# A transformer block on one core: the second chunk of x loaded ahead of wk and w_mod, silu on GpSimd, a copied w_phi product, and a new order

## The chip, the cores and the metric

The kernel runs on one core of a Trainium2 chip. The metric is the device time in microseconds, the median of several runs. The core has five instruction streams that wait for each other through semaphores: TensorE (PE, with its weight loads PEld), VectorE (DVE), ScalarE (ACT), GpSimd (POOL) and SyncE (SP), which here issues nearly all DMAs.

## The reference

Only the computation is shown; all inputs and outputs are bf16, and S = 2048 tokens, D = 512, 32 heads of 16, F = 1376.

```python
mod = (silu(c) @ w_mod).reshape(1, 6, 1, 512)        # sa, ca, ga, sb, cb, gb
h = layernorm(x) * (1 + ca) + sa
x = x + ga * A(h)
h = layernorm(x) * (1 + cb) + sb
x = x + gb * (silu(h @ w_gate) * (h @ w_up)) @ w_down

def A(h):
    q, k, v = heads(h @ wqkv)
    pq, pk = q @ w_phi, k @ w_phi                    # one 16x16 matrix for each head
    phi_q = concat(softmax(pq), softmax(-pq)); phi_k = concat(softmax(pk), softmax(-pk))
    kv = sum over tokens of phi_k^T v; z = sum over tokens of phi_k
    return ((phi_q @ kv) / (phi_q @ z + 1e-6)) @ wo
```

## The kernel before

The 2048 tokens are 4 chunks (x_c0 to x_c3) of 4 tiles of 128 tokens; the 16 tiles are numbered through. All weights stay in SBUF once loaded.

Preparation. x, wk, w_phi and w_mod are loaded by `later` (L288), one DMA on SP each. silu(c) is computed in `f_silu` (L453) with an Exp before it (L459). Its product with w_mod (`mod_cols`, L465) gives the shift and scale columns modA (and later modB and the gates). w_phi is folded into wk and wq: `f_phx` (L495) spreads the heads' matrices into PSUM, one product with a mask (L502) makes the block matrix BD of it, and `fold_phi` (L508) turns wk by TensorE (L519), evacuates the turned pieces WT (L523), multiplies them with BD (L530), and evacuates the result over wk (L533, L534). wq is turned by DMA instead. First layernorm (`first_norm`, L542): statistics by VectorE (L348, L349), the reciprocal root either by Ln and Exp on ScalarE (L377, L378) or by GpSimd (L381, L382), a small reduction (L384), and the normalization on one of three engines (L392, L396, L398). Tiles 0 to 5 are turned by TensorE (L563, L414), later ones by DMA (L577); the evacuation applies modA and gives hT (L566, L567 for tiles 0 and 1, L422 for tiles 2 to 5).

First phase. For each tile `k_tile` computes K (L619) and V (L623) into PSUM banks. Two Exp of K on ScalarE (L634) give e, VectorE sums them (S, L640), R is the reciprocal, va is V times R (L650), GpSimd scales e (L657), and eight small matmuls add to kv (L663). `q_tile` does the like for Q (L686, L690, L694, L701), whose result goes through a DMA transpose (pT, L705).

Second phase. For each tile kv is applied (L824), the denominators are inverted (A, L827), the result o is turned (oT), multiplied with wo (L857, whose columns were scaled by the gate at L780), added to x, normalized again and turned; then the gated feed-forward network (L909, L916 to L926, L955) and the product with w_down (L987), the last sum (L997, L1001) and the store (L1007).

The order of all this isn't the order of the code. Each piece is registered by `pl.op` with the engine or engines that may do it and a duration. A list of numbers, `ORDER`, fixes in which sequence they are placed and which engine does each: a number is four times the operation's index plus the choice among its engines. From the durations `Plan.run` computes planned starts, and the instructions are issued sorted by them, so each engine's own sequence is fixed in the program:

```python
for x in ORDER:
    o = self.ops[x // 4]
    o.alt = o.alts[x % 4]
...
for o in sorted(self.ops, key=lambda o: (o.start, o.n)):
    if o.eng == "PE":
        fill(last, o, fns)
```

`fill` (L1037) puts matmuls of ones (L1054) into planned gaps of TensorE; their results are not used. Six PSUM banks of 512 columns (`one_ps`) are shared by nearly all products, so a product may have to wait until an earlier one in its bank has been read.

Of the kernel before, what the change touches and what calls it, by code (L numbers as in the profile page):

```python
# [14 lines left out]
P = 128  # L15
# [5 lines left out]
D = 512  # L21
# [14 lines left out]
def fm_size(m):  # L36
# [5 lines left out]
DMA_LN1 = 6  # L42
FILL_FROM, FILL_TO, FILL = 1.3, 90.0, 0.85
# [3 lines left out]
    0, 4, 48, 188, 72, 80, 8, 12, 16, 76, 20, 60, 52, 204, 228, 84, 56, 220, 172, 64, 208, 89, 92, 98, 156, 232, 176, 224, 24, 212, 104, 180, 193,  # L47
    28, 161, 236, 100, 184, 240, 196, 108, 217, 40, 246, 112, 164, 148, 116, 120, 124, 153, 36, 250, 32, 200, 268, 140, 168, 132, 128, 276, 316,
    252, 272, 68, 260, 144, 280, 136, 520, 264, 256, 324, 285, 320, 524, 328, 44, 424, 488, 428, 288, 560, 528, 464, 380, 492, 333, 600, 568, 294,
    298, 480, 432, 300, 472, 484, 336, 564, 468, 476, 368, 496, 342, 308, 532, 436, 346, 536, 304, 500, 541, 392, 440, 348, 608, 312, 384, 548, 445,  # L50
    604, 572, 510, 388, 828, 768, 404, 577, 452, 772, 544, 872, 372, 820, 376, 812, 776, 1344, 584, 506, 552, 513, 940, 518, 448, 460, 408, 412,
    804, 362, 358, 456, 396, 580, 780, 366, 944, 816, 864, 354, 904, 596, 824, 400, 868, 556, 808, 640, 832, 636, 612, 785, 792, 592, 836, 840, 908,
    788, 617, 644, 588, 1020, 876, 704, 800, 1340, 858, 1028, 648, 1024, 950, 796, 624, 881, 916, 620, 652, 416, 629, 962, 953, 888, 632, 860, 958,
    853, 1060, 921, 736, 656, 912, 1032, 846, 1188, 884, 712, 708, 900, 928, 716, 964, 1037, 744, 1228, 1268, 740, 1276, 924, 660, 1044, 850, 896,
    1308, 748, 1304, 933, 1040, 664, 1192, 1232, 893, 1200, 1360, 420, 1052, 936, 1318, 668, 720, 988, 1272, 1056, 993, 1240, 1196, 1049, 752, 1352,
    1205, 1325, 1212, 1328, 1208, 1224, 1280, 1313, 1236, 1322, 1245, 1252, 1336, 1356, 1220, 1285, 1364, 1248, 1264, 724, 1520, 1600, 1217, 1524,
    1369, 1292, 1604, 1528, 1260, 1348, 1004, 1560, 728, 1257, 1288, 1372, 1297, 1532, 1300, 1008, 1376, 1608, 1612, 1384, 1537, 1544, 1540, 1564,
    1816, 1388, 1617, 1620, 1640, 968, 1552, 1381, 1644, 1572, 1556, 1064, 1549, 1624, 1652, 1577, 1632, 1568, 1124, 1584, 1332, 1132, 1128, 1648,
    1580, 1592, 1596, 972, 1657, 1136, 976, 672, 1660, 1068, 996, 1636, 1589, 756, 1664, 1629, 1672, 732, 1072, 1669, 1676, 676, 1824, 980, 760,
    1828, 1092, 680, 1001, 1832, 1100, 984, 1680, 1836, 684, 1856, 1860, 1096, 1076, 1812, 1864, 1156, 1104, 1108, 1160, 1808, 1744, 2164, 1820,  # L60
    2168, 764, 1080, 1084, 2172, 1868, 1872, 1392, 1164, 1876, 1400, 2176, 688, 1748, 1424, 1112, 1116, 1880, 2180, 1688, 2184, 1488, 692, 1088,
    1884, 1396, 1712, 1888, 1120, 2416, 1684, 2188, 1140, 696, 1168, 1432, 1892, 2420, 700, 1752, 1776, 2424, 1716, 1898, 1172, 1456, 1492, 1144,
    1496, 1148, 1012, 1720, 1908, 1428, 1912, 1464, 2428, 1900, 1904, 2432, 2216, 1176, 2192, 2436, 2220, 2224, 2196, 2012, 2440, 1784, 2228, 1936,
    1152, 2016, 1460, 1180, 1780, 2200, 1016, 2204, 1952, 1500, 1916, 2020, 2232, 1940, 1944, 1956, 2237, 1948, 2444, 2208, 2024, 1404, 1960, 1184,
    2214, 2468, 2028, 1436, 2512, 2516, 1964, 1920, 1968, 2240, 1504, 2032, 2520, 2257, 1988, 2472, 2250, 1972, 2524, 1992, 1408, 1976, 2448, 1440,
    2246, 2253, 2296, 1980, 2528, 2316, 1924, 2452, 2036, 1984, 2260, 2040, 2532, 1444, 2304, 1412, 1448, 1416, 1452, 2352, 2536, 2044, 2300, 2456,
    1928, 2476, 2324, 2320, 1508, 1420, 1788, 2048, 2460, 2280, 2328, 1692, 2936, 1512, 1932, 2052, 2264, 2308, 2480, 2284, 2940, 2540, 2268, 2272,
    2288, 2944, 2056, 1516, 2332, 2544, 2484, 2924, 2360, 2564, 2292, 1848, 2928, 2340, 2932, 1792, 2948, 2064, 2568, 2548, 2312, 2060, 2336, 1724,
    2552, 2490, 2368, 2068, 2344, 2088, 2465, 1996, 2356, 2104, 2572, 2576, 2348, 2392, 1696, 2364, 2976, 2580, 2000, 2128, 2096, 1468, 1472, 2585,
    2072, 2556, 1728, 2980, 1476, 2492, 2984, 2372, 2276, 2506, 2112, 1732, 2124, 1481, 2952, 1756, 2988, 2561, 2588, 2510, 2132, 3032, 3036, 2605,  # L70
    1700, 1484, 3040, 2594, 2956, 1796, 2376, 2396, 2092, 2498, 1704, 2400, 2601, 2108, 2501, 2597, 2992, 1736, 2136, 2076, 3020, 2380, 2704, 2808,
    3024, 2080, 2720, 3028, 2960, 2404, 2116, 2997, 2964, 2668, 2648, 2816, 2100, 3044, 2724, 1708, 2652, 1760, 2728, 1740, 2732, 2968, 2676, 2974,
    2664, 2672, 3072, 2680, 3048, 3076, 3444, 1764, 2656, 2712, 2812, 2736, 3080, 3000, 2608, 2120, 3448, 2756, 1801, 3452, 2820, 3432, 3052, 3084,
    1804, 3056, 2760, 2744, 3060, 2140, 2660, 2764, 2824, 2628, 2612, 3436, 2616, 3064, 3088, 2408, 2144, 3013, 3006, 3440, 2700, 2620, 2084, 3094,
    3009, 2772, 2768, 2708, 2740, 1768, 3069, 3456, 2632, 3540, 3096, 2004, 2780, 1853, 2776, 3544, 2784, 2716, 3460, 2148, 3105, 2152, 3484, 3101,
    3017, 3548, 3488, 3492, 2792, 2684, 1772, 2636, 2688, 2748, 3464, 3114, 3528, 3532, 3110, 2752, 2788, 3536, 2692, 3468, 2640, 3552, 2796, 3116,
    3472, 2800, 3268, 3264, 3212, 3220, 2008, 3272, 2696, 3120, 2804, 3136, 3140, 3496, 3208, 3500, 3276, 3144, 3556, 3560, 3172, 3244, 3564, 3216,
    3476, 3568, 2624, 3482, 3180, 3148, 3300, 2900, 3580, 3572, 3584, 3176, 3252, 2156, 3224, 2904, 3308, 2876, 3124, 2852, 3588, 3506, 3184, 2644,
    2412, 3592, 2880, 2884, 2385, 2908, 3508, 3284, 3152, 2912, 3188, 3304, 2856, 3292, 3280, 3248, 3596, 3312, 3602, 3525, 3192, 3256, 3578, 3288,
    3604, 3200, 2860, 3617, 1844, 3296, 3196, 3128, 3228, 3514, 3613, 3236, 3320, 3316, 2388, 3156, 3608, 3521, 3620, 1841, 3518, 3204, 2864, 3160,  # L80
    3132, 3716, 3164, 2888, 3232, 3720, 3260, 3168, 3240, 3664, 3644, 3324, 3328, 3648, 3684, 3728, 3384, 3332, 3692, 3652, 2160, 3336, 3724, 3388,
    3672, 2828, 3360, 3408, 3392, 3412, 2868, 2832, 3364, 3396, 3656, 3340, 3788, 3624, 3416, 3344, 2917, 3732, 3368, 2872, 3401, 2893, 2836, 2840,
    3796, 2920, 3628, 3632, 3668, 3420, 3756, 3636, 3404, 3700, 2844, 3808, 3708, 2848, 3676, 3348, 3680, 3688, 3704, 3712, 3792, 3764, 3752, 3776,
    3760, 3812, 3372, 3696, 3772, 3800, 3740, 3816, 3736, 3376, 3768, 2896, 3780, 3824, 3804, 3660, 3424, 3828, 3380, 3744, 3748, 3784, 3844, 3848,
    3892, 3640, 3836, 3820, 3916, 3920, 3832, 3840, 3852, 3924, 3353, 3896, 3900, 3356, 3868, 3872, 3876, 3928, 3856, 3940, 3944, 3948, 3861, 3960,
    3964, 3968, 3933, 3904, 3428, 3909, 3864, 3880, 3952, 3936, 3912, 3885, 3972, 3976, 3956, 3888,
# [122 lines left out]
def kernel(  # L209
# [78 lines left out]
    def later(dst, src, w, kb):  # L288
        pl.op("XBAR", w=list(w), us=0.5, kb=kb, fn=lambda: nc.sync.dma_start(dst, src))
# [25 lines left out]
    nc.gpsimd.memset(mhalf[:], -0.5)  # L315
    eps_t = const.tile([P, 1], FP32, name="eps")
# [114 lines left out]
    later(x_ch[0][:], x_v[0], bx[0:4], 400)  # L431
# [32 lines left out]

    def mod_cols(mt, n0, bw):  # L465
# [69 lines left out]

    hT = [[attn.tile([P, CW], BF16, name=f"hT_{c_i}_{j}") for j in range(KD)] for c_i in range(NCH)]
    bhT = [[[Buf() for _ in range(KD)] for _ in range((2, 2, 1, 1)[c_i])] for c_i in range(NCH)]

    bxn1 = {}
    bmodA = None  # L540

# [552 lines left out]
```

## Time and profile before

| | |
|---|---|
| time, median of 3 runs | 199.34 us (199.23 to 199.69) |
| time of the profiled execution | 199.18 us |
| its span in the profile | 197.4 us |
| granted TensorE clock | 1.00 |
| TensorE busy | 192.4 us, 97% of the span |
| VectorE, ScalarE, GpSimd busy | 136.3, 108.9, 126.0 us |
| moved by DMA | 24.16 MB |

The span reaches from the first to the last recorded instruction; the time also holds what lies around it. A row of the timeline gives the start in us, the duration of the group in us, the engine, the line, the operation, what it writes and reads, the shape, and how many instructions were merged. In brackets stands how long the engine had been idle and what released it. Ends of matmuls are modelled, so I count a row of matmuls by its starts. Busy columns of the windows view are PE, PEld, VectorE, ScalarE and GpSimd, then the granted clock, the DMA engines' share and the GB/s moved.

### The profile page before, as it was taken

What the parts mean: (1) busy time and instruction counts of PE and PEld (TensorE: products, weight loads), DVE (VectorE), ACT (ScalarE), POOL (GpSimd) and SP (SyncE); (2) the same over time, 40 slices, a digit from 0 to 9 for tenths busy, and PEclk for the clock granted to TensorE, in tenths of its full rate; (3) what the DMA queues carried; (4) which work ended last, traced back from release to release, by engine and by line L of the source; (5) the groups of instructions that cost most, each with busy time, mean ns of one, the idle gap of its engine ahead of it and who ended that gap; (6) DMA issues with size and microseconds to landing.
All of it is one profiled execution on the core that took longest, in us unless ns stands there. A gap on an engine that the chain in (4) does not pass through costs nothing.

```text
span 197.4 us, 4080 instructions
## 1 busy us (share of the span) xinstructions
PE 192.4 (97%) x1494; PEld 108.1 (55%) x1494; DVE 136.3 (69%) x268; ACT 108.9 (55%) x247; POOL 126.0 (64%) x207
## 2 busy tenths in 40 slices
PE   7999999999999999999999999999999999999993
PEld 2754555555754777967664555554444544544452
DVE  5999999999999899998973873844234203241453
ACT  2499999999769974366452452633145330134300
POOL 1469999999997667686763777657746420139200
DMA  6999789899928570836509157150370001021112
GB/s 203 334 381 151 129 201 355 186 310 392 203 53 162 107 151 13 167 66 110 99 14 188 37 100 82 30 130 0 66 103 20 27 0 53 3 66 40 47 38 76
DMA packets 51141, 24.16 MB, mean 122 GB/s; under 512 B 42449, under 2 KB 47922, under 8 KB 51122
## 3 DMA queue, kind: packets, MB, share of 16 engines
q1 hardware_dynamic: 50976, 23.88, 51.7%
q8 instruction: 11, 0.18, 0.4%
q14 instruction: 8, 0.07, 0.1%
q10 hardware_dynamic: 146, 0.03, 0.1%
HBM read 11.58 MB, written 2.10 MB: 69 GB/s over the span
## 4 chain that ended last, share of the span: by engine, by line
PE 93%; DMA 3%; DVE 1%; issue 1%; SPq 0%; DVEq 0%
PE one_ps L909 35%; PE one_ps L987 17%; PE one_ps L857 7%; PE one_ps L623 7%; PE one_ps L686 7%; PE one_ps L619 7%; PE one_ps L955 3%; DMA wk<-in_A_wqkv_dram 2%; PE kv_ps L663 2%; PE kv_ps L824 2%; PE kv_ps L1054 1%; DMA out_dram<-ot 1%; PE one_ps L530 1%; PE one_ps L473 1%; DVE fg L997 1%; PE one_ps L414 1%
## 5 line engine op out<-in xcount | busy, mean ns | idle before, releaser
L909 PE MATMUL one_ps<-hT,wgu_sb 128*128 128x512 bf16 (+2 forms) x480 | 74.5, 308 | 0.0
L909 PEld LDWEIGHTS <-wgu_sb 128*128 128x128 bf16 x480 | 40.3, 98 | 28.7
L916 ACT ACTIVATE sg<-one_ps 128x512 bf16<-128x512 f32 (+1 forms) x41 | 23.6, 586 | 37.2 <-PE one_ps L909 24.9
L987 PE MATMUL one_ps<-wd_sb,gu 128*128 128x512 bf16 (+1 forms) x160 | 37.8, 372 | 0.0
L925 POOL TENSOR_TENSOR gu<-usb,sg 128x512 bf16<-128x512 bf16 x19 | 22.1, 1168 | 24.2 <-ACT sg L916 12.2
L997 DVE TENSOR_TENSOR fg<-one_ps,gab 128x512 bf16<-128x512 f32 (+1 forms) x16 | 10.4, 667 | 23.8 <-PE one_ps L987 23.8
L919 DVE TENSOR_TENSOR gu<-one_ps,sg 128x512 bf16<-128x512 f32 (+1 forms) x22 | 14.2, 658 | 18.1 <-PE one_ps L909 11.1
L987 PEld LDWEIGHTS <-gu 128*128 128x128 bf16 x180 | 16.6, 98 | 16.0
L348 DVE BATCH_NORM_STATS2 st<-x_c 128x6 f32<-128x512 bf16 x32 | 21.3, 678 | 1.7 <-DMA x_c<-in_A_x_dram 1.5
L923 ACT CAST usb<-one_ps 128x512 bf16<-128x512 f32 x19 | 11.1, 586 | 18.2 <-PE one_ps L909 18.0
L640 DVE TENSOR_REDUCE S<-e 128x64 f32<-128x1024 bf16 x16 | 19.2, 1202 | 0.4 <-POOL e L657 0.2
L694 DVE TENSOR_REDUCE Sq<-eq 128x64 f32<-128x1024 bf16 x16 | 19.2, 1203 | 0.0
L690 ACT ACTIVATE eq<-one_ps 128x512 bf16<-128x512 f32 x32 | 17.1, 614 | 2.3 <-PE one_ps L686 2.2
L634 ACT ACTIVATE e<-one_ps 128x512 bf16<-128x512 f32 x32 | 17.0, 615 | 0.0
L657 POOL TENSOR_TENSOR e<-e,S 128x512 bf16<-128x512 bf16 x16 | 16.8, 1060 | 0.2
L857 PE MATMUL one_ps<-wo_sb,oT 128*128 128x512 bf16 x64 | 16.1, 379 | 0.0
L623 PE MATMUL one_ps<-wv,hT 128*128 128x512 bf16 x64 | 15.9, 379 | 0.0
L619 PE MATMUL one_ps<-wk,hT 128*128 128x512 bf16 x64 | 15.5, 379 | 0.0
L686 PE MATMUL one_ps<-wq,hT 128*128 128x512 bf16 x64 | 15.4, 379 | 0.0
L701 POOL TENSOR_TENSOR eq<-eq,Rq 128x512 bf16<-128x512 bf16 x14 | 14.8, 1059 | 0.4
L1001 POOL TENSOR_TENSOR ot<-x_c,fg 128x512 bf16<-128x512 bf16 x7 | 8.1, 1153 | 10.0 <-DVE fg L997 10.0
L860 DVE TENSOR_TENSOR x_c<-x_c,one_ps 128x512 bf16<-128x512 bf16 x16 | 10.7, 669 | 5.3 <-PE one_ps L857 5.1
(120 smaller groups left out, 279.7 us busy)
## 6 DMA issues: line engine op xcount, KB each, us to landing
wmod_sb<-in_w_mod_dram SPq DMA_DIRECT2D x2, 1024.0 KB, 7.8
out_dram<-ot SPq DMA_DIRECT2D x15, 128.0 KB, 1.9
x_c<-in_A_x_dram SPq DMA_DIRECT2D x3, 512.0 KB, 7.2
wgu_sb<-in_B_w_up_dram SPq DMA_DIRECT2D x1, 1376.0 KB, 10.9
wgu_sb<-in_B_w_gate_dram SPq DMA_DIRECT2D x1, 1376.0 KB, 13.4
wd_sb<-in_B_w_down_dram SPq DMA_DIRECT2D x1, 1280.0 KB, 7.5
wk<-in_A_wqkv_dram SPq DMA_DIRECT2D x1, 512.0 KB, 4.8
wmod_sb<-in_w_mod_dram SPq DMA_DIRECT2D x1, 512.0 KB, 5.9
```

What stands on the lines that cost most here:

```text
L348: pl.op("DVE", r=reads, w=[st6], us=0.6, fn=lambda: nc.vector.bn_stats(st6()[:], src))
L619: nc.tensor.matmul(pk()[:], lhsT=hT[c_i][k][:, cols], rhs=Wk2[:, k, :], start=(k == 0), stop=(k == KD - 1))
L623: nc.tensor.matmul(v()[:], lhsT=hT[c_i][k][:, cols], rhs=wv_sb[:, k, :], start=(k == 0), stop=(k == KD - 1))
L640: pl.op("DVE", r=[e], w=[Ss], us=1.13, fn=lambda: nc.vector.tensor_reduce(Ss()[:].rearrange("p g s h -> p (g s h)"), e()[:].rearrange("p g ...
L686: nc.tensor.matmul(pq()[:], lhsT=hT[c_i][k][:, cols], rhs=Wq2[:, k, :], start=(k == 0), stop=(k == KD - 1))
L690: pl.op("ACT", r=[pq, btab], w=[be[sg]], us=0.48, fn=lambda sg=sg: nc.scalar.activation(eq[:, :, sg].rearrange("p g h f -> p g (h f)"), pq ...
L694: pl.op("DVE", r=be, w=[Sq], us=1.13, fn=lambda: nc.vector.tensor_reduce(Sq()[:].rearrange("p g s h -> p (g s h)"), eq[:].rearrange("p g s ...
L857: nc.tensor.matmul(a()[:], lhsT=oT()[:, j0 + j, :], rhs=wo_sb[:, j, :], start=(j == 0), stop=(j == KD - 1))
L909: nc.tensor.matmul(ps_()[0:fsz, q * n:(q + 1) * n], lhsT=wgu_sb[:, k, i, m * P:m * P + fsz], rhs=h2[k], start=(k == 0), stop=(k == KD - 1))
L916: pl.op("ACT", r=[g, btab], w=[sg], us=0.08 + 0.41 * L / CW, fn=lambda: nc.scalar.activation(sg()[0:fsz, 0:L], g()[0:fsz, 0:L], ACT.Silu))
L925: pl.op("POOL", r=[usb, sg], w=[gu], us=0.17 + 0.98 * L / CW, fn=lambda: nc.gpsimd.tensor_tensor(gu()[0:fsz, 0:L], usb()[0:fsz, 0:L], sg() ...
L987: nc.tensor.matmul(fp()[:], lhsT=b()[0:fsz, c0:c0 + P], rhs=wd_[0:fsz, m, wcs], start=(m == 0), stop=(m == FM - 1))
```

## The change

The first chunk of x is loaded in two halves, and the order of the loads on SP becomes: first chunk, second chunk (in halves, as before), wk, w_phi, w_mod, third chunk, wq, fourth chunk, wv. In the kernel before it is: first chunk, wk, w_phi, w_mod, second chunk, third chunk, wq, wv, fourth chunk.

silu(c) is computed by GpSimd, as c times (1 + exp(-c)) to the power -1, from an SBUF copy of c that ScalarE makes. The spread w_phi is copied from PSUM to SBUF, and the block matrix is the product of this copy with the mask. It may be done by GpSimd or VectorE; `ORDER` takes VectorE for the copy and for the product. For tile 0 the reciprocal of the denominators may be done by ScalarE as Exp of minus Ln, and `ORDER` takes that. A function for layernorm statistics on ScalarE is added, but the tuple that would select tiles for it, `ACT_STATS`, is empty.

`ORDER` is new throughout. From it follow, among others: all four evacuations of tiles 0 and 1 on VectorE (L567) instead of one there and three on ScalarE; the reciprocal roots of tiles 0 to 7 by Ln and Exp on ScalarE instead of those of tiles 2 and 3 only; three of the turned pieces of wk evacuated by ScalarE instead of two; K of tiles 0 to 4 ahead of the first V instead of K of tiles 0 to 3; four transposes of the second chunk ahead of the first K; 23 filler matmuls instead of 26, of them two behind the first K instead of five; w_up's load behind the third transposed eq instead of behind the first.

```diff
+ACT_STATS = ()
+ACC = 0.8
+EARLY = 1
...
 ORDER = [
...
+    mone = const.tile([P, KD], FP32, name="mone")
+    nc.gpsimd.memset(mone[:], -1.0)
...
-    later(x_ch[0][:], x_v[0], bx[0:4], 400)
+    later(x_ch[0][:, 0:2, :], x_v[0][:, 0:2, :], bx[0:2], 210)
+    later(x_ch[0][:, 2:4, :], x_v[0][:, 2:4, :], bx[2:4], 190)
...
+    c_sb = const.tile([P, KD], FP32, name="c_sb")
+
+    def f_sig():
+        nc.scalar.copy(c_sb[:], cT()[:])
+        nc.scalar.activation(sig[:], cT()[:], ACT.Exp, scale=-1.0)
+
     def f_silu():
-        nc.vector.tensor_scalar_add(sig[:], sig[:], 1.0)
-        nc.vector.reciprocal(rsig[:], sig[:])
-        nc.vector.tensor_tensor(silucT[:], rsig[:], cT()[:], op=ALU.mult)
+        nc.gpsimd.tensor_scalar(sig[:], sig[:], 1.0, 1e38, op0=ALU.add, op1=ALU.min)
+        nc.gpsimd.tensor_tensor(rsig[:], sig[:], mone[:, 0:KD], op=ALU.pow)
+        nc.gpsimd.tensor_tensor(silucT[:], rsig[:], c_sb[:], op=ALU.mult)
...
-    pl.op("ACT", r=[cT], w=[bsig], us=0.1, fn=lambda: nc.scalar.activation(sig[:], cT()[:], ACT.Exp, scale=-1.0))
-    pl.op("DVE*", r=[bsig, cT], w=[bsil], us=0.5, fn=f_silu)
+    pl.op("ACT", r=[cT], w=[bsig], us=0.3, fn=f_sig)
+    pl.op("POOL", r=[bsig], w=[bsil], us=1.5, fn=f_silu)
...
-    pl.op("DVE", r=[phx], w=[bBD], us=0.6, fn=lambda: nc.vector.tensor_tensor(
-        BD[:], phx()[:].rearrange("p (j f) -> p j f", f=DH).unsqueeze(2).to_broadcast([P, KD, 8, DH]),
-        bm128[:].unsqueeze(1).to_broadcast([P, KD, 8, DH]), op=ALU.mult))
+    ph_sb = prep.tile([P, KD * DH], BF16, name="ph_sb")
+    bph = Buf()
+    pl.op([("ACT", 0.14, lambda: nc.scalar.copy(ph_sb[:], phx()[:])),
+           ("DVE", 0.13, lambda: nc.vector.tensor_copy(ph_sb[:], phx()[:]))], r=[phx], w=[bph])
+
+    def f_bd(eng):
+        eng.tensor_tensor(BD[:], ph_sb[:].rearrange("p (j f) -> p j f", f=DH).unsqueeze(2).to_broadcast([P, KD, 8, DH]),
+                          bm128[:].unsqueeze(1).to_broadcast([P, KD, 8, DH]), op=ALU.mult)
+    pl.op([("POOL", 1.05, lambda: f_bd(nc.gpsimd)), ("DVE*", 0.6, lambda: f_bd(nc.vector))], r=[bph], w=[bBD])
...
-        pl.op("DVE", r=[nd], w=[A], us=0.26, fn=lambda: nc.vector.reciprocal(A()[:], ndv()[:, :, HG:NDW]))
+        alts = [("DVE", 0.26, lambda: nc.vector.reciprocal(A()[:], ndv()[:, :, HG:NDW]))]
+
+        def fa():
+            nc.scalar.activation(A()[:], ndv()[:, :, HG:NDW], ACT.Ln)
+            nc.scalar.activation(A()[:], A()[:], ACT.Exp, scale=-1.0)
+        if n < EARLY:
+            alts.append(("ACT", 0.43, fa))
+        pl.op(alts, r=[nd] + ([btab] if n < EARLY else []), w=[A])
```

## The prediction

> **What bounds the kernel now.** I read the page first (part 1 for shares, part 4 for the chain), then the chain in order of time, then the timeline of the first 20 us, the DMA issues, and the busy time by window.
>
> ```profile
> span 197.4 us, 4080 instructions
> PE 192.4 (97%) x1494; PEld 108.1 (55%) x1494; DVE 136.3 (69%) x268; ACT 108.9 (55%) x247; POOL 126.0 (64%) x207
> PE 93%; DMA 3%; DVE 1%; issue 1%; SPq 0%; DVEq 0%
> ```
>
> TensorE is on the chain for 93% of the span. From the first K matmul on, it is a row of matmuls:
>
> ```profile
> 1.18 4.83 DMA wk<-in_A_wqkv_dram
> 10.53 0.83 PE kv_ps L1054 x4
> 12.35 1.73 PE one_ps L619 x8
> 14.16 1.73 PE one_ps L619 x8
> 16.05 0.97 PE one_ps L623 x4
> ```
>
> The chain begins with the load of wk, passes the preparation, and enters K (L619) at about 12.2 us. A 128x512 matmul is started every 0.216 us (8 in 1.73). The changed kernel issues the same matmuls apart from the fillers (L1054, products of ones that only keep the array busy). So the end is: start of the first K, plus matmul work left, plus fillers and waits after it, plus a tail whose instructions are alike in both (last matmul 193.97, span 197.4). In the timeline:
>
> ```profile
> 8.20 0.30 ACT L377 ACTIVATE ln_var<-ln_mv,eps 128x2 f32<-128x2 f32 x1
> 9.07 1.56 ACT L533 CAST wk<-one_ps 128x512 bf16<-128x512 f32 x3 [0.34 <-PE one_ps L530]
> 10.21 0.17 DVE L478 COPY modA<-one_ps 128x8 f32<-128x8 f32 x1 [0.48 <-PE one_ps L473]
> 10.51 1.50 ACT L566 ACTIVATE hT<-one_ps,modA 128x256 bf16<-128x256 bf16 x3
> 12.19 1.89 PE L619 MATMUL one_ps<-wk,hT 128*128 128x512 bf16 x8
> 15.73 0.32 PE L1054 MATMUL kv_ps<-ones 128*128 128x373 bf16 x1
> 15.99 1.02 PE L623 MATMUL one_ps<-wv,hT 128*128 128x512 bf16 x4
> 16.85 0.61 PE L414 MATMUL one_ps<-ident_b,xn 128*128 128x128 bf16 x8
> ```
>
> The first K waits for ScalarE, which evacuates wk until about 10.5 and then three of the four turned pieces of h one after the other. Counting the later starts against 0.216 us each, I find little else lost: five fillers after 12.19 (191, 373, 512, 480 and 228 columns, together 1784, that is 0.75 us), 0.10 before V at 15.99, 0.10 before the first product with wo at 58.5, and some 0.6 us in pieces. What can be won after the start is 1.5 us at most.
>
> ```profile
> wk<-in_A_wqkv_dram SPq DMA_DIRECT2D x1, 512.0 KB, 4.8
> wmod_sb<-in_w_mod_dram SPq DMA_DIRECT2D x2, 256.0 KB, 6.2
> 8.00:9.00 1.00, 1.00 (x21) 0.87 (x20) 1.00 (x6) 0.69 (x3) 0.77 (x1) 1.00 1.05 391
> 9.00:10.00 1.00, 1.00 (x34) 1.00 (x32) 0.72 (x3) 0.93 (x2) 0.77 (x2) 1.00 1.06 404
> ```
>
> wk lands at 6.0, the last quarter of w_mod at about 9.5; the queue moves 391 to 404 GB/s then (last column), without a gap.
>
> **The change part by part.**
>
> *Second chunk of x ahead.* SP's order becomes x0a, x0b, x1a, x1b, wk, w_phi, w_mod, x2, wq, x3, wv. 512 KB pass ahead of wk: 524 KB by 391 GB/s is 1.34 us. So wk lands at 7.35, w_phi at 7.5, the end of w_mod at 10.8. The bytes ahead of x2 and wq are unchanged (about 12.1 and 13.6). x3 and wv swap: wv lands where x3 did, about 17.3 instead of 15.95. SP issues take 0.4 to 0.7 us each, at most eight in flight. With the load of c as the first, the ninth waits for c and the tenth for x0a; both have landed by 4, so no issue is late.
>
> *First chunk in halves.* One issue more (0.45 us on SP). The first half should land near 3.5 instead of 4.1. The Trainium skill ("DMA: Bandwidth & Descriptors", sections "Anatomy of one DMA" and "Measured") speaks against it: it gives a DMA (measured on the GpSimd path) a fixed cost of about 2 us and asks for 1 MiB or more. The row says otherwise here: quarters of w_mod of 256 KB landed 0.7 us apart in the filled queue, which is their bytes at the rate above. By the rule taken serially, the half would add up to 2 us to all loads behind it (first K near 14.7); by the row, nothing. I take the row, since the fixed part is latency that lies under the transfers ahead.
>
> *silu on GpSimd.* Three VectorE instructions go (138+178+157 ns, 0.47 us); ScalarE gains a copy of c (0.17). GpSimd gets an add (0.23, row L381), a pow (0.72 for 128x2, L382; this one is 128x4, so 0.7 to 0.9) and a product (0.2, L332). It starts near 3.9 and ends by 5.3. Its reader, w_mod's products, waits for w_mod until 9.5, so it costs nothing; without that cover it would cost 0.9 us more than VectorE's version. Queued behind it on GpSimd are the masks and the first normalization, which can't start before 6.8.
>
> *w_phi's block matrix.* A copy of 128x64 on VectorE (bound 0.13 to 0.3 by the small copies; I take 0.15) and a product from SBUF, still on VectorE. The old product from PSUM took 0.673. The nearest row with two SBUF inputs is L701 on VectorE: 1011 ns. The skill ("GPSIMD Engine Reference", "Specifications") says that VectorE contends with GpSimd for SBUF when it has two SBUF inputs. The page gives no price, so the row sets it: between 0.67 and 1.01 us, I take 1.0. It ends near 9.4; ScalarE reaches wk only at 10.0. So either value gives the same sum.
>
> *Start of K, new order.* ScalarE decides. The second group of wk's turned pieces is ready for it at 8.5 (7.35, two groups of 0.23, w_phi's 0.45 between, a handover of 0.2, a little issue). Then: two WT copies of 0.48, a Ln/Exp pair 0.53 (0.30+0.20 and the gap), two wk copies of 0.48 (three in 1.44 by starts), a second pair 0.53: 11.48. VectorE waits for this pair in the reduction in front of the h pieces: handover 0.2, 0.14, then the two pieces at 0.33 (0.41 less the overlap seen between VectorE starts): 12.48. Handover 0.18: first K at 12.66, 0.47 later than 12.19. w_mod's last product (10.8) gives modA by 11.5, earlier than that. All four pieces of tiles 0 and 1 are now on VectorE. ScalarE does tiles 2 and 3 meanwhile, done near 13.8; K needs them at 14.2. Tiles 4 and 5 are done by 16.6, before K reaches them at 16.7.
>
> *What comes back.* Four transposes of the second chunk now lie ahead of the first K: 8 took 0.45 by starts, so -0.22. Fillers after the first K: 512 and 219 columns, 731 for 1784: -0.44. The wait for wv: five K tiles now come first, so V is due at 17.5, after 17.3: -0.10. At the first wo, 1.17 us instead of 0.87 of other matmuls lie under the copy of oT: -0.10. The reciprocal of tile 0's denominators by Ln and Exp on ScalarE costs 0.52 (0.266+0.256, rows L644 and L645) against 0.34, in front of a VectorE product; 1.6 us of other matmuls lie over both: nothing, or 0.2 if they don't suffice.
>
> *GpSimd's row.* A second row must keep up: GpSimd works from the first normalizations of later tiles to the last product with e, and the last kv matmuls stand right behind it.
>
> ```profile
> 14.88 3.79 POOL L398 TENSOR_SCALAR xn<-x_c,ln_mv,ln_nmr 128x512 bf16<-128x512 bf16 x5
> 51.85 1.06 POOL L657 TENSOR_TENSOR e<-e,S 128x512 bf16<-128x512 bf16 x1
> ```
>
> By starts, that row is 37.6 us of work and 0.4 idle. In the new order eight normalizations are done ahead, and from the first one of x2 to the last product with e there are 34.6 us (normalization 0.75, product 1.02, the small ones about 0.2). It starts when VectorE has reduced x2's statistics. That reduction is queued behind the sum S of the first K tile, which waits for its Exp: ScalarE is at 15.6, S ends at 16.9, statistics of x3 take 0.6, the reduction 0.15: 17.65. 17.65+34.6+0.4 = 52.65 against 52.9: -0.25. VectorE has about 1 us less in this phase, ScalarE 0.3 more; there I enter nothing, with -0.6 to +1.5 for the range.
>
> *Weights.* w_up's load is now queued behind the third transposed eq on SP instead of ahead of it. Its transfer takes 11 us, its reader starts near 67; the third eq is ready before 50 by GpSimd's row. It costs nothing unless it is issued after 55.
>
> Sum: to the last kv the array's own row gives +0.47 -0.22 -0.44 -0.10 = -0.29 and GpSimd's -0.25; the later one counts. With the wait at wo: -0.25 -0.10 = -0.35. The profiled execution took 199.18 (span 197.4 and 1.78 around it), 0.16 below the median of 199.34. 199.18 - 0.35 = 198.83; on the median's level 198.99, given as 199.0.
>
> **The rivals.** *Slower: preparation follows wk.* If ScalarE's row from wk to the h pieces shrinks by nothing, the first K is late by the whole 1.34: +1.34 -0.22 -0.44 -0.20 = +0.48, 199.8. For it: the chain starts at wk, and this order puts two Ln/Exp pairs between the copies. Against: three h pieces (1.35) leave ScalarE ahead of the first K. It decides once the first K is later than about 13.05.
>
> *Slower: GpSimd late.* The first Exp now ends near 15.6 instead of 14.7, and x2's normalization hangs on it. If ScalarE or the wait for x2's statistics puts it 1.2 us later than computed, 18.85, the last kv is 0.95 later than before, less 0.10: +0.85, 200.2. Against: the gaps in front of it are filled by computed work, not by guesses. It decides from 17.9 on.
>
> *More gain.* wk lands 0.2 earlier, and the 0.6 us of waits in pieces shrink because VectorE has 1 us less: -0.35 -0.6: 198.4.
>
> *No change.* An x half that lands no earlier than the whole, or 0.2 us more at two handovers, uses up the sum: about 199.3.
>
> **How the numbers follow.** About 0.2% (0.4 us) is what a measurement of this kernel can tell from no change. The forecast has an own range of 198.5 to 199.4 and the chance 0.46; its centre is near that border: 0.25 faster, 0.18 same, 0.03 slower. More gain 0.19, all faster. Following wk 0.20: 0.03 same, 0.17 slower. GpSimd late 0.15: 0.02 same, 0.13 slower. No change is the upper half of the first case. Together 0.44, 0.23 and 0.33. The range from 198.0 to 200.5 leaves out about 0.1 on either side.
>
> **What would show it.** Right: wk landing near 7.4, w_mod's end near 10.8, the first K at 12.5 to 12.8, two fillers behind it, V without a wait near 17.5, x2's first normalization at 17.5 to 17.9. Wrong: a first K past 13; V waiting for wv; Exp instructions holding banks for which K or V waits between 18 and 30 us; the block matrix's product ending after 9.8.

## The result and the profile after

The changed kernel takes 201.91 us (median of 4 runs, 201.63 to 202.26), the kernel before 199.51 beside it: a ratio of 1.0114, interval 1.0076 to 1.0151. It is 2.4 us slower. The profiled execution took 201.69 with a span of 199.9 us, 2.5 more than before, at the same granted clock of 1.00.

Parts 1 and 4 of the page after (the last line gives the chain's shares by engine):

```profile
span 199.9 us, 4067 instructions
PE 191.7 (96%) x1467; PEld 108.0 (54%) x1491; DVE 137.4 (69%) x265; ACT 111.7 (56%) x255; POOL 127.0 (64%) x206
PE 77%; DMA 9%; DVE 5%; POOL 4%; issue 2%; SPq 1%; POOLq 0%
```

TensorE is busy no longer than before (191.7 against 192.4 us) and the span is 2.5 us longer: the array waits more. Its share of the chain fell from 93% to 77%, DMA's rose from 3% to 9%. The chain in order of time (start, duration, engine, what) says where:

```profile
2.58 6.27 DMA wk<-in_A_wqkv_dram
13.38 0.69 DVE hT L603 x2
15.13 3.02 PE one_ps L655 x14
18.46 0.86 PE one_ps L655 x4
19.32 1.73 PE one_ps L659 x8
...
97.75 4.76 DMA pT<-eq
```

wk (forecast at 7.35) lands at 2.58 + 6.27 = 8.85 instead of 6.0, and a transposed eq, which no chain had before, stands in it near 100 us. The timeline after:

```profile
8.89 0.40 PE L537 MATMUL one_ps<-ident_b,wk 128*128 128x128 bf16 x4 [1.45 <-DMA wk<-in_A_wqkv_dram]
13.35 1.50 DVE L603 TENSOR_SCALAR hT<-one_ps,modA 128x256 bf16<-128x256 bf16 x4
14.53 0.38 PE L655 MATMUL one_ps<-wk,hT 128*128 128x512 bf16 x1
17.99 0.47 PE L1097 MATMUL kv_ps<-ones 128*128 128x512 bf16 x2
19.16 1.24 PE L659 MATMUL one_ps<-wv,hT 128*128 128x512 bf16 x5
19.44 0.78 POOL L403 TENSOR_SCALAR xn<-x_c,ln_mv,ln_nmr 128x512 bf16<-128x512 bf16 x1 [0.47 <-issue]
```

TensorE turns wk (L537) as soon as it is there. Of its 1491 matmuls (as many as weight loads) 1467 have a record. The first K is among the missing; its weight load starts at 14.21. So I take the first K from the weight loads in all kernels: 12.07 before, 14.21 after, 2.14 later.

For waits behind it I use the starts of the rows of matmuls, 0.216 us for 512 columns and the smaller ones in proportion; what passes beyond that is a wait. From 24 us to the end this gives 0.71 us before and 1.90 after, of which 0.68 between 60 and 67 us and 0.80 between 90 and 105. The count after is uncertain by some 0.2 us, because a missing record has to be filled in. The waits view of TensorE for 56 to 106 us (line, what it waited for, us in total, times, longest) is empty for the kernel before, and after it reads:

```profile
PE kv_ps L860 <- DMA pT<-eq: 0.6, 1, 0.6
PE one_ps L419 <- POOL xn L403: 0.2, 1, 0.2
```

The sum: +2.14 for the first K, -0.22 for four transposes now ahead of it, -0.44 for fillers, -0.10 for V without a wait, 1.90 - 0.71 = +1.19 for later waits, together +2.57. The span grew by 2.5. So there are two losses: a late first K, behind a late wk, and an order that leaves TensorE waiting late in the kernel. The experiments separate them.

### The profile page after: what moved, and what is told of

Same layout as the page of the kernel before. It is cut to its first block, busy times and chain, and to the rows that moved or that the text cites. A ratio compares the mean times of both kernels' runs of the same rounds, so it can differ in the third digit from the quotient of the medians.

```text
span 199.9 us, 4067 instructions
## 1 busy us (share of the span) xinstructions
PE 191.7 (96%) x1467; PEld 108.0 (54%) x1491; DVE 137.4 (69%) x265; ACT 111.7 (56%) x255; POOL 127.0 (64%) x206
## 4 chain that ended last, share of the span: by engine, by line
PE 77%; DMA 9%; DVE 5%; POOL 4%; issue 2%; SPq 1%; POOLq 0%
PE one_ps L952 33%; PE one_ps L1030 17%; PE one_ps L655 6%; PE one_ps L900 6%; PE one_ps L659 6%; DMA wd_sb<-in_B_w_down_dram 3%; DMA wk<-in_A_wqkv_dram 3%; DMA pT<-eq 2%; PE one_ps L998 2%; PE one_ps L722 2%; DVE o L871 1%; PE kv_ps L860 1%; PE kv_ps L699 1%; PE one_ps L548 1%; POOL ln_rstd L365 1%
## 5 line engine op out<-in xcount | busy, mean ns | idle before, releaser
L1040 DVE TENSOR_TENSOR fg<-one_ps,gab 128x512 bf16<-128x512 f32 (+1 forms) x16 | 10.6, 669 | 23.9 <-PE one_ps L1030 22.6
L966 ACT CAST usb<-one_ps 128x512 bf16<-128x512 f32 x19 | 11.1, 584 | 17.9 <-PE one_ps L952 14.8
L923 ACT ACTIVATE hT<-raw,modB 128x256 bf16<-128x256 bf16 x20 | 11.4, 592 | 13.8 <-DMA raw<-xn 13.8
L1044 POOL TENSOR_TENSOR ot<-x_c,fg 128x512 bf16<-128x512 bf16 (+1 forms) x10 | 11.1, 1123 | 10.7 <-DVE fg L1040 10.7
L693 POOL TENSOR_TENSOR e<-e,S 128x512 bf16<-128x512 bf16 x16 | 17.3, 1078 | 0.2
L900 PE MATMUL one_ps<-wo_sb,oT 128*128 128x512 bf16 x61 | 15.9, 379 | 0.2
L737 POOL TENSOR_TENSOR eq<-eq,Rq 128x512 bf16<-128x512 bf16 x15 | 15.9, 1065 | 0.2
```

Source lines behind the costliest of these rows:

```text
L693: pl.op("POOL", r=[e, Ss], w=[e], us=1.02, fn=lambda: nc.gpsimd.tensor_tensor(e()[:, :, 1], e()[:, :, 1], Ss()[:, :, 0].unsqueeze(3).to_br ...
L900: nc.tensor.matmul(a()[:], lhsT=oT()[:, j0 + j, :], rhs=wo_sb[:, j, :], start=(j == 0), stop=(j == KD - 1))
```

## The experiments

| kernel | us, median (range, runs) | ratio to before (95%) | wk lands | first K | waits after 24 us |
|---|---|---|---|---|---|
| before | 199.2 to 199.5 | 1 | 6.01 | 12.07 | 0.71 |
| after | 201.91 | 1.0114 (1.0076-1.0151) | 8.85 | 14.21 | 1.90 |
| b_x1_first | 202.72 (202.64-203.29, 4) | 1.0175 (1.0150-1.0200) | 8.80 | 16.3 | 0.71 |
| a_wk_first | 203.35 (202.10-204.01, 6) | 1.0185 (1.0151-1.0219) | 7.70 | 15.9 | - |
| a_whole | 200.71 (200.46-201.39, 6) | 1.0072 (1.0051-1.0093) | 7.38 | 13.04 | 1.67 |
| a_wphi_behind | 204.73 (202.93-205.31, 6) | 1.0256 (1.0219-1.0292) | 8.82 | 17.0 | - |
| b_halves | 199.82 (199.26-201.88, 22) | 1.0025 (1.0013-1.0037) | 6.77 | 12.8 | about 0.8 |
| b_silu_bd | 199.39 (198.91-199.91, 14) | 1.0001 (0.9989-1.0013) | 5.65 | 12.1 | - |
| b_head_a_tail | 203.44 (202.79-203.90, 5) | 1.0192 (1.0173-1.0210) | 5.77 | 12.1 | see text |
| a_head_b_tail | 201.92 (201.73-202.84, 5) | 1.0137 (1.0118-1.0157) | 7.39 | 13.1 | see text |
| b_wk_halves | 199.47 (198.78-203.40, 22) | 1.0008 (0.9992-1.0025) | see text | see text | - |
| b_x0_rows | 200.46 (200.15-200.53, 5) | 1.0058 (1.0046-1.0070) | 6.72 | 13.2 | about 0.6 |
| b_head_a_tail2 | 200.68 (200.42-200.84, 5) | 1.0068 (1.0055-1.0081) | 5.93 | 12.0 | 1.84 |
| a_head_b_tail2 | 199.74 (199.56-200.50, 8) | 1.0029 (1.0018-1.0040) | 7.88 | 13.24 | 0.95 |
| a_swap_sp | 201.01 (200.67-203.31, 6) | 1.0103 (1.0066-1.0140) | 8.13 | 13.5 | see text |
| a_swap_both | 200.62 (200.53-200.90, 6) | 1.0068 (1.0052-1.0084) | 7.75 | 13.1 | see text |
| a_best | 202.76 (202.61-203.34, 5) | 1.0183 (1.0162-1.0204) | 5.64 | 14.5 | - |
| b_x1_fill | 201.60 (201.08-202.31, 6) | 1.0114 (1.0089-1.0139) | 9.01 | 15.1 | - |

wk's landing and the first K are those of one profiled execution. Landings scatter: four kernels whose loads are those of before have wk at 5.65 to 6.01, five with the loads of a_whole at 7.38 to 8.13. "-" is not evaluated.

### The loads: b_x1_first, a_wk_first, a_whole, a_wphi_behind

`b_x1_first` is the kernel before, with x1's halves issued ahead of wk:

```diff
+LOADS = (0, 6, 7, 1, 2, 3, 4, 5, 10, 9, 8, 11)
-        for o in sorted(self.ops, key=lambda o: (o.start, o.n)):
+        fns += [self.ops[n].alt[2] for n in LOADS]
+        for o in sorted(self.ops[len(LOADS):], key=lambda o: (o.start, o.n)):
```

> The kernel before with one edit: SP issues the two halves of x1 ahead of wk, w_phi and w_mod; every engine's own row of instructions is that of before. Theory 1 (the load of x1 ahead of wk makes the loss): wk lands at 7.4 by its bytes alone (6.0 + 1.34), up to 8.9 if the rate sags as it does in the changed kernel; the first K moves by as much, +1.4 to +2.9, and nearly all of it reaches the end: 200.7 to 202.2. Theory 2 (the changed order of the engines makes the loss, by the waits behind 60 us): wk lands just as late, but the old order soaks it up behind the first K, and the time stays below 200.1 (under +0.6).

`a_wk_first` is the changed kernel with wk ahead of x1 and w_phi behind it, and `a_wphi_behind` puts w_phi behind the first piece of w_mod:

```diff
+LOADS = (0, 1, 2, 7, 8, 3, 4, 5, 6, 11, 10, 12, 9)
```
```diff
+LOADS = (0, 1, 7, 8, 2, 4, 3, 5, 6, 11, 10, 12, 9)
```

> The changed kernel with one edit: wk is issued behind x0's halves and ahead of x1's; all else as it was. Theory 1: wk lands near 6, that is 2.8 earlier; x1 lands 1.3 later, and VectorE, which has x1's statistics ahead of w_phi's copy, is held until about 10, so the first K comes 0.8 to 2 earlier and the time is 200.0 to 201.1. Theory 2 (waits of the new order): the first K comes earlier as well, but the later waits eat it: within 0.4 of 201.9.

> The changed kernel with w_phi's load (16 KB in rows of 128 bytes) issued behind the first half of w_mod instead of between wk and w_mod. If w_phi's short rows cause the low rate ahead of wk's landing (in the kernel before a gap of 0.9 us stands where w_phi passes), wk lands at 7.4 to 7.9 instead of 8.85; w_phi itself lands about 1.3 later than wk, so the block matrix is no earlier than now, and the time changes by -0.6 to +0.3. If not, wk stays at 8.7 to 9.0, and the time is the same or up to 0.8 longer since the block matrix waits for w_phi.

`a_whole` is the changed kernel with x0 and x1 as one DMA each, the same bytes in the same order:

```diff
-    later(x_ch[0][:, 0:2, :], x_v[0][:, 0:2, :], bx[0:2], 210)
-    later(x_ch[0][:, 2:4, :], x_v[0][:, 2:4, :], bx[2:4], 190)
+    later(x_ch[0][:], x_v[0], bx[0:2], 210)
...
-    for t in (0, 2):
-        later(x_ch[1][:, t:t + 2, :], x_v[1][:, t:t + 2, :], bx[TPC + t:TPC + t + 2], 270)
+    later(x_ch[1][:], x_v[1], bx[TPC:TPC + 2], 270)
```

> The changed kernel with x0 and x1 loaded by one DMA each (4 KB rows, two transfers) instead of two each (2 KB rows, four transfers). If the halves cause the low rate (150 to 350 GB/s from 3.1 to 7.3 us in the changed kernel, where 391 was counted on), the rate is near 390 and wk lands at 7.4 to 7.6 instead of 8.85; the first K follows by 1.0 to 1.4, time 200.5 to 201.0. If the halves are not the cause, wk still lands at 8.5 to 9.0 and the time is within 0.4 of 201.9; x0's statistics, 0.8 later, cost nothing in either case.

`a_whole` is the clearest of the four. The time falls by 1.0 us, from 2.40 over its kernel before to 1.44; the two intervals overlap at their edges, but the slowest of its runs (201.39) is below the fastest of after (201.63). wk lands at 7.38, and at no more than 8.13 in the four other kernels with these loads, instead of 8.85 (8.82 in a_wphi_behind, which has the same halves). So the cut into halves, with the bytes unchanged, cost about 1 us.

Windows of 3.5 to 6.5 us, first after, then a_whole:

```profile
3.50:4.50 1.00, 1.00 (x4) 0.38 (x4) 1.00 (x2) 0.24 (x2) 0.54 (x2) 1.00 0.81 209
4.50:5.50 1.00, 1.00 (x3) 0.30 (x2) 0.89 (x4) 0.00 (x0) 0.92 (x3) 1.00 0.90 309
5.50:6.50 1.00, 1.00 (x4) 0.39 (x3) 1.00 (x4) 0.50 (x2) 0.74 (x6) 1.00 0.92 295
```
```profile
3.50:4.50 1.00, 1.00 (x4) 0.37 (x4) 0.39 (x1) 0.24 (x2) 0.54 (x2) 1.00 1.00 401
4.50:5.50 1.00, 1.00 (x3) 0.30 (x2) 1.00 (x4) 0.00 (x0) 0.92 (x3) 1.00 0.92 304
5.50:6.50 1.00, 1.00 (x4) 0.40 (x3) 1.00 (x3) 0.26 (x1) 0.73 (x6) 1.00 1.10 362
```

With the halves the queue moves 209 GB/s where it moves 401 with whole chunks. In these 3 us that is 0.81 MB against 1.07 MB, and up to 7.38 us, where wk lands in a_whole, 1.59 against 1.95 MB (means of 215 and 264 GB/s): 0.9 us at 391 GB/s. The rest of the 1.5 is not rate: when wk lands in after, at 8.85, 2.15 MB have passed, 0.2 MB more than in a_whole, so more of the later loads had gone by before wk was complete.

Each DMA also takes SP about 0.45 us, so wk is issued later, at 2.58 instead of 1.64. That alone is not the price: in b_x1_fill wk was issued 0.77 us later than in b_x1_first (2.88 and 2.11) and landed 0.2 later.

`b_x1_first` shows the loads without the new order, with x0 whole and x1 in halves: wk lands at 8.80, nearly as late as in the changed kernel, the waits after 24 us are the old 0.71, and it is slower still. From wk's landing to the first K matmul pass 7.6 us there instead of 6.2 before; b_x1_fill below tells why.

`a_wk_first` and `a_wphi_behind` are misses of mine. The new order has VectorE reduce x1's statistics ahead of the block matrix. With w_phi at 9.3 and 10.4 the block matrix came at 10.6 and later, the clock fell to 0.50, and K began at 15.9 and 17.0. Their times show that this order depends on its order of loads, and not what an early wk is worth.

For the queue `a_wk_first` has a hint: I expected wk near 6, and it landed at 7.70, although the bytes ahead of it and its issue (1.64) are those of b_halves, where it landed at 6.77. What differs stands behind wk: x1's halves instead of w_phi and w_mod.

### The halves alone: b_halves, b_wk_halves, b_x0_rows

All three are the kernel before, with one load cut in two:

```diff
-    later(x_ch[0][:], x_v[0], bx[0:4], 400)
+    def two_halves():
+        for t in (0, 2):
+            nc.sync.dma_start(x_ch[0][:, t:t + 2, :], x_v[0][:, t:t + 2, :])
```
```diff
-    later(Wk2[:], wqkv_v[:, :, D:2 * D], bwk[0:1], 690)
+    def two_halves():
+        for k in (0, 2):
+            nc.sync.dma_start(Wk2[:, k:k + 2, :], wqkv_v[:, k:k + 2, D:2 * D])
```
```diff
-    later(x_ch[0][:], x_v[0], bx[0:4], 400)
+    def two_halves():
+        for h in (slice(0, 64), slice(64, 128)):
+            nc.sync.dma_start(x_ch[0][h], x_v[0][h])
```

> The kernel before with x0 loaded as two halves (2 KB rows) instead of one DMA; all else as it was. Theory (in the traces so far the rate falls once the first two transfers of the queue are through, to 150 to 350 GB/s, so small transfers at the front starve it): wk is now the third transfer and lands at 6.6 to 7.2 instead of 6.0; the first K follows, 199.9 to 200.5. Rival (only x1's 512 KB ahead of wk count, halves of x0 are harmless): wk at 6.0 to 6.2, time 199.1 to 199.6.

> The kernel before with wk loaded by two DMAs of 256 KB (two of its four blocks of rows each; rows of 1 KB as before) instead of one; x0 is whole. Reason A (small transfers at the front of the queue cost time each, whatever they read): wk's second half lands at 6.4 to 6.9 instead of 6.0, time 199.6 to 200.2. Reason B (it is x read in 2 KB pieces that is slow): 6.0 to 6.2, time 199.2 to 199.6.

> The kernel before with x0 loaded by two DMAs of 64 partitions each, so that the rows stay 4 KB, instead of one; the loads behind it are as before. Reason A (each small transfer costs): wk lands at 6.5 to 7.0 as with halves of 2 KB rows (6.75), time 199.6 to 200.2. Reason B (the 2 KB pieces): wk at 6.0 to 6.2, time 199.2 to 199.6.

`b_halves`: no byte more ahead of wk, yet wk lands at 6.77 and the median is 0.42 us up, a small loss, whose interval (1.0013 to 1.0037) leaves out 1. The window of 3.5 to 4.5 us of b_halves, then of before:

```profile
3.50:4.50 1.00, 1.00 (x4) 0.38 (x4) 1.00 (x2) 0.17 (x1) 0.00 (x0) 1.00 0.86 230
```
```profile
3.50:4.50 1.00, 1.00 (x4) 0.38 (x4) 0.37 (x1) 0.17 (x1) 0.00 (x0) 1.00 1.04 334
```

The rate is 230 GB/s instead of 334. `b_x0_rows` keeps a row of x in one piece of 4 KB, on 64 partitions each: slow too (second half 5.26, wk 6.72). So it is not the length of the row alone; but such a half may be slow for its 64 partitions, which this run can't separate.

`b_wk_halves` is inconclusive: the ratio of 1.0008 is not clear of 1 (0.9992 to 1.0025). Its profiled execution, with wk at 7.08, took 201.65 and is no typical run. A good part of its 2.3 us is the clock, in this row:

```profile
8.00 1.44 PE L522 MATMUL one_ps<-ident_b,wk 128*128 128x128 bf16 x12
```

Twelve turnings in 1.44 us are half rate (0.83 at full rate, see b_x1_fill below), although the windows view gives 1.00 here. So halves of wk show no certain price, halves of x do, and why x as two transfers of 256 KB costs more than as one of 512 KB stays open.

### silu and the block matrix: b_silu_bd

The kernel before with silu on GpSimd, the copy of c on ScalarE, and the block matrix from an SBUF copy, all in the old places of the order:

```diff
+        nc.gpsimd.tensor_tensor(rsig[:], sig[:], mone[:, 0:KD], op=ALU.pow)
...
+        nc.vector.tensor_copy(ph_sb[:], phx()[:])
```

> The kernel before with silu on GpSimd (with the copy of c on ScalarE) and w_phi's block matrix from a copy in SBUF, at the same places of the order. Theory: both are harmless, 199.0 to 199.7, the block matrix's product takes 0.66 us beside GpSimd as in the changed kernel. Rival (these pieces make part of the loss: GpSimd is late with x0's normalization, or the product is slowed to 1.0 us): 199.9 to 200.6.

The ratio is 1.0001: nothing, as forecast. In its timeline the power is the longest of GpSimd's three instructions, and the product is as short as the one from PSUM (0.67):

```profile
4.22 1.05 POOL L463 TENSOR_TENSOR rsig<-sig,mone 128x4 f32<-128x4 f32 x1
7.14 0.69 DVE L514 TENSOR_TENSOR BD<-ph_sb,bm 128x512 bf16<-128x512 bf16 x1
```

### The order, cut in two: b_head_a_tail, a_head_b_tail and again with other seams

One kernel takes `ORDER` of before up to a planned time and that of the change behind it, the other the reverse on top of a_whole. The first pair has its seam at 40 us, in mid phase; the second at 68 and 54 us.

```diff
-ORDER = [
...
+ORDER = [
...
```

> The kernel before with its own order of work up to about 40 us and the changed kernel's order behind that; loads, silu and block matrix as before. Theory 2 (the new order has waits of its own behind 45 us): the first K stays at 12.2, yet 0.7 to 1.2 us of new stalls lie behind 45 us: 200.0 to 200.6. Rival (those waits only follow from the late start): 199.0 to 199.6.

> The changed kernel with whole loads of x0 and x1 (200.7), its own order up to about 40 us and the order of the kernel before behind that. Theory 2: the stalls behind 45 us go, 199.5 to 200.1. Rival (they follow from the late start): within 0.3 of 200.7.

> As the run before with the old order ahead and the changed order behind, with the seam moved to about 68 us, where the two orders stand at the same work (the seam at 40 cost 1.5 us of its own). Theory 2 says that the changed order has a wait of its own between 90 and 105 us (0.6 to 1.0 in every trace that has this tail): 199.9 to 200.4. Rival: 199.2 to 199.6.

> The changed kernel with whole loads of x0 and x1 (200.7), its own order up to about 54 us, where the last kv product stands, and the old order behind it (the seam at 40 cost some 2 us of its own). Theory 2: the waits at 60 to 67 (0.6) and 90 to 105 (0.6) go: 199.5 to 200.0. Rival (they follow from the late start): 200.4 to 201.0.

The seam at 40 us made waits of its own: 1.0 us and 0.5 of fillers between 36 and 52 us in the one, 1.2 and 1.5 between 36 and 60 in the other. Their times (203.44 and 201.92) say little; only that the latter, behind its seam, waited just 0.3 us in all from 60 us on. The second pair is cleaner. b_head_a_tail2 starts K on time and still loses 1.4 us:

```profile
12.11 1.89 PE L615 MATMUL one_ps<-wk,hT 128*128 128x512 bf16 x8
100.82 0.43 PE L820 MATMUL kv_ps<-KVZ,pT 128*128 128x68 bf16 x8 [0.45 <-DMA pT<-eq]
```

TensorE's waits between 90 and 106 us:

```profile
PE kv_ps L820 <- DMA pT<-eq: 0.5, 1, 0.5
PE one_ps L951 <- POOL hT L878: 0.3, 1, 0.3
```

a_head_b_tail2, whose waits view for 56 to 106 us is empty, is 1.0 us faster than a_whole (ratios 1.0029 and 1.0072), although its first K is no earlier (13.35, and 13.36 in a_whole):

```profile
13.35 0.59 PE L651 MATMUL one_ps<-wk,hT 128*128 128x512 bf16 x2
```

So the order behind 54 us costs about 1 us by itself, with the intervals of the two kernels apart (1.0018 to 1.0040 and 1.0051 to 1.0093).

### Which instruction of the tail: a_swap_sp, a_swap_both

a_whole with two transposed eq exchanged on SP, so that the one TensorE waits for goes first; then also with a product of GpSimd ahead of two scalings of wo's columns:

```diff
+        a, b = self.ops[429], self.ops[437]
+        a.start, b.start = b.start, a.start
+        self.ops[273].start = self.ops[455].start - 0.001
```

> The changed kernel with whole loads (200.7) and two neighbours on SP exchanged: the transposed eq of tile 13, which TensorE reads at about 101 us, is issued ahead of that of tile 12, which it reads at 104; all else as it was. If SP's order makes the waits at 100 to 103, they shrink from 0.6 to 0.2 or less: 200.2 to 200.5. If they come from the later transposed h (raw from xn, issued behind both), the time stays within 0.2 of 200.7.

> The run above with one more exchange: on GpSimd the product for eq of tile 4 goes ahead of two scalings of wo instead of behind them (2.2 us earlier; the last scaling ends as before). If GpSimd's order makes the wait at 65 us (0.6: TensorE waits for the first normalized x of the second part, which stands behind VectorE's work for these tiles), that wait goes too: 0.3 to 0.6 below the run above. If not, the same as the run above, or slower if wo's first product now waits.

Neither helped (1.0103 and 1.0068 against a_whole's 1.0072; the 1.0103 holds one run of 203.31 us at a mean clock of 0.989, its median is 201.01 against 200.71). The waits between 56 and 106 us of a_whole, a_swap_sp and a_swap_both:

```profile
PE one_ps L419 <- POOL xn L403: 0.4, 1, 0.4
PE kv_ps L860 <- DMA pT<-eq: 0.2, 1, 0.2
```
```profile
PE one_ps L421 <- POOL xn L405: 0.5, 1, 0.5
PE one_ps L1000 <- POOL hT L927: 0.3, 1, 0.3
```
```profile
PE kv_ps L863 <- DVE x_c L906: 0.3, 1, 0.3
PE one_ps L1001 <- POOL hT L928: 0.3, 1, 0.3
```

With one supplier hurried, TensorE waits for the next one: the transpose, then GpSimd's hT, then VectorE's sum. That suggests a tail that is late on several rows at once; which instruction would have to move first stays open.

### A version meant to beat both: a_best

The order of a_head_b_tail2, with loads x0, wk, w_phi, x1, w_mod, and a head by hand: x1's statistics behind the block matrix, wk's evacuations ahead of the third Ln and Exp, two h pieces on ScalarE.

```diff
-ORDER = [
...
+ORDER = [
...
```

> The changed kernel with whole loads, the old order behind 54 us (199.74 so far), and a new order ahead: SP issues x0, wk, w_phi, x1, w_mod; x1's statistics on VectorE stand behind w_phi's block matrix, wk's copies on ScalarE ahead of the third Ln/Exp pair, and the last two pieces of h of the first tiles go to ScalarE. Theory 1: wk lands at 6.0 to 6.3 again, the end of w_mod at 10.8, modA near 11.5, so the first K starts near 12.3 instead of 13.4 and the time is 198.5 to 199.2, below the kernel before. Rival (x1's statistics, now later, hold GpSimd's normalizations and so the row to the last kv product): no better than 199.5.

It lost 3.5 us. wk landed at 5.64, but my order made K late, by 2.45 us (14.52 instead of 12.07):

```profile
7.21 1.12 DVE L516 TENSOR_TENSOR BD<-ph_sb,bm 128x512 bf16<-128x512 bf16 x1
14.33 1.02 ACT L598 ACTIVATE hT<-one_ps,modA 128x256 bf16<-128x256 bf16 x2 [1.10 <-PE one_ps L595]
```

ScalarE's two h pieces waited 1.1 us for their transposes (L595). An early wk is worth nothing if the first layernorm then comes late. Where the other microsecond went stays open.

### The clock: b_x1_fill

b_x1_first with six fillers of 512 columns ahead of wk's first turning:

```diff
+            if o.n == 47:
+                left += 6 * CW
```

> The kernel before with x1's two halves ahead of wk, and six more fillers of 128x512 ahead of wk's first turning, so that TensorE is not idle between 5.9 and 8.4 us. If the halved clock made the further 1.4 us between wk's landing and K, the clock stays at 1.00, the first K matmul starts at 15.0 to 15.2 us instead of 16.44 and the time is about 201.3 us. Rival, the copies and their order made it: the first K matmul still starts after 16 us, 202.7 us.

The timeline and the windows of 9 to 10 us of b_x1_first, then of b_x1_fill:

```profile
8.85 0.61 PE L521 MATMUL one_ps<-ident_b,wk 128*128 128x128 bf16 x4 [2.91 <-DMA wk<-in_A_wqkv_dram]
9.72 1.44 PE L521 MATMUL one_ps<-ident_b,wk 128*128 128x128 bf16 x12
16.44 1.89 PE L621 MATMUL one_ps<-wk,hT 128*128 128x512 bf16 x8
9.00:10.00 1.00, 1.00 (x24) 1.00 (x22) 0.09 (x1) 0.00 (x0) 0.00 (x0) 0.50 1.07 412
```
```profile
9.06 0.40 PE L521 MATMUL one_ps<-ident_b,wk 128*128 128x128 bf16 x4 [1.82 <-DMA wk<-in_A_wqkv_dram]
9.70 0.83 PE L521 MATMUL one_ps<-ident_b,wk 128*128 128x128 bf16 x12
15.19 1.89 PE L621 MATMUL one_ps<-wk,hT 128*128 128x512 bf16 x8
9.00:10.00 1.00, 0.94 (x26) 0.94 (x27) 0.12 (x1) 0.00 (x0) 0.00 (x0) 1.00 1.05 412
```

Though wk landed 0.2 later, K starts 1.25 us earlier and the median is 1.1 us lower. So b_x1_first's further loss was the clock: the twelve turnings of its second group take 1.44 us at 0.50 and 0.83 at 1.00. The changed kernel itself doesn't pay this: its planned order puts more fillers there, TensorE idled for 1.45 us ahead of wk, and the clock stayed at 1.00.

The length of one gap is not what decides. In a_wk_first the clock fell as well, with no gap as long as 1.45 us:

```profile
7.75 0.40 PE L539 MATMUL one_ps<-ident_b,wk 128*128 128x128 bf16 x4 [0.82 <-DMA wk<-in_A_wqkv_dram]
9.33 0.58 PE L513 MATMUL one_ps<-wphi_sb,spread 128*128 128x16 bf16 x16 [1.19 <-DVE ln_mv L356]
10.00:11.00 1.00, 1.00 (x10) 0.77 (x8) 1.00 (x5) 0.93 (x3) 1.00 (x3) 0.50 1.04 421
```

## Why the prediction was wrong

The forecast was 0.35 us faster, the outcome 2.4 slower. Two terms entered as nothing were each about a microsecond, and the first K would have been about half a microsecond later than forecast even without them.

*"By the row, nothing" (halves): the first failed step.* I set wk's landing at 7.35: 1.34 for the bytes and nothing for the size. With whole chunks wk landed at 7.38 to 8.13 in five kernels, so what the bytes alone give is the best case and not the typical one; with the halves it landed at 8.82 and 8.85, and the medians put the price of the halves at about 1.0. The row I had taken, quarters of w_mod 0.7 us apart, belongs to a queue already full. x1's halves are not new; new is that they stand at the front of the queue, and there I had no row. Against the row I had weighed the Trainium skill ("DMA: Bandwidth & Descriptors", "Anatomy of one DMA"), which gives about 2 us of fixed cost for a DMA on the GpSimd path; by an estimate that takes this serially the first K came near 14.7. Measured were 14.3 for the first matmul. The rule's direction was right here and mine wrong. Its size is not what the runs show: x0's second transfer alone moved wk by 0.76 us in b_halves, not by 2.

*From wk's landing to the first K: right, but only for a late wk.* Forecast 5.31, after 5.46 (to the matmul, 0.1 behind its weight load), and 5.47 in a_head_b_tail2 and both swaps. Where wk was earliest, in a_whole and a_head_b_tail, it was 5.8, and the first K came at 13.15 and not at 12.66. The chain of a_whole up to its first K does not hold wk's load. It passes VectorE's statistics, GpSimd's first normalizations, and their transposes (L599), which this order puts ahead of the last group of wk's turnings (L537):

```profile
6.63 0.68 DVE st L353
7.47 1.53 POOL xn L403 x2
9.05 0.23 PE one_ps L599
9.28 0.22 PE one_ps L537 x4
```

So "ScalarE decides" left out a second row, which set the first K in these two kernels, 0.5 us later than the sum had it. 13.15 is also beyond the 13.05 that I gave as the point from which the rival "preparation follows wk" decides. With both other losses taken out, in a_head_b_tail2, 0.44 us remain (199.74 against 199.3), where that rival said 0.48. Its size came out; its reason, ScalarE's row, is not what the chain of a_whole shows.

*"There I enter nothing" (later waits): the second failed step.* I had given it -0.6 to +1.5 for the range and zero in the sum. It is +1.19 by the starts after, and in the medians 1.0 (a_head_b_tail2) and 1.4 us (b_head_a_tail2) by the two kernels with the order cut. It was not the phase I looked at (GpSimd's row, 15 to 53 us) but the second phase, for which I had checked one wait, the first product with wo, and one load.

*GpSimd late: the event came, the effect didn't.* x2's first normalization starts at 19.44, past the 17.9 from which that rival should decide. But between 24 and 52 us TensorE loses only 0.16 us: with K itself 2.1 us late, GpSimd's row no longer sets the end of the phase. This rival isn't the cause.

*What held.* Two fillers (17.99), V without a wait (19.16), four transposes ahead of the first K, silu and the block matrix at nothing. I had taken 1.0 for the block matrix's product, for VectorE's contention with GpSimd; it takes 0.66 after and 0.69 in b_silu_bd. The contention came all the same, but GpSimd paid it: after, its normalization that starts at 10.10, 0.09 behind the product, takes 1.21 us instead of 0.77. In a_best a normalization started first, at 7.02, and the product, from 7.21 on, takes 1.12. In b_silu_bd no normalization ran beside it. The forecast said that either value gives the same sum, and b_silu_bd bears it out.

The range ended at 200.5. It had room for one of the two microseconds, not for both.

## What to carry to other kernels

A row that prices a transfer holds for its place in the queue: before a load is split or moved to the front, look for the price of a transfer at the front, and with none, enter both ends in the sum's range, not only in the text. When a whole order is replaced, every phase is changed: a term "nothing" has to be supported by each phase's own waits, and two kernels with the order cut at a phase boundary (not in mid phase) show afterwards which part pays. If a load on which TensorE waits is moved back, the array's idle time grows with it, and fillers have to be moved too, or the clock may fall, which cost another 1.1 us in b_x1_first. And a start may be set by a second row that stands just behind the first: with wk early, the statistics and normalizations of the first layernorm decided.

## What the runs showed of the hardware

- TensorE idle for 2.91 us (5.94 to 8.85, b_x1_first): clock 0.50 from about 8.86 to 12.26 us (worked out from means of 0.93, 0.50 and 0.87 in the windows 8 to 9, 9 to 12 and 12 to 13). Idle for 1.82 us (b_x1_fill) or 1.45 us (after): 1.00. But in a_wk_first two gaps of 0.82 and 1.19 us sufficed: 0.50 from about 9.38 to 12.80 (means of 0.69, 0.50 and 0.60 in 9 to 10, 10 to 12 and 12 to 13). By the windows view TensorE was busy for 1.4 of the 3.4 us ahead of that fall, and for 1.8 of the 3.4 us up to 8.86 in b_x1_fill, where it did not fall. The Trainium skill ("TensorE: Matmul & The Clock Gate", "What's actually happening" in Part 1) gives about 3.4 us of idle time for the fall and as much busy time for the return. Here less sufficed for the fall; both stretches at 0.50 lasted 3.4 us, which agrees.
- The column of the granted clock is not enough at the start of a kernel: it reads 1.00 while ten fillers of 512 columns take 4.00 us (after, from 3.45), most of them 0.43 us apart by their starts instead of 0.216.
- x in transfers of 256 KB at the front of SP's queue: 209 and 230 GB/s from 3.5 to 4.5 us in after and b_halves, against 401 and 334 with whole chunks (a_whole, before).
- VectorE's product of two SBUF inputs (128x512) and a GpSimd normalization that overlap: one of them takes about 0.44 us longer (the normalization 1.21 instead of 0.77 in after, the product 1.12 instead of 0.66 to 0.69 in a_best).
- GpSimd's power takes 1.05 us for 128x4 and 0.72 for 128x2; I had estimated 0.7 to 0.9.
